# Wider token groups in the gated stage of a one-core attention and expert kernel

## The chip, the core and the metric

The kernel runs on one core of a Trainium2 chip. Its engines are TensorE (PE in the profile; its weight loads are PEld), VectorE (DVE), ScalarE (ACT), GpSimd (POOL) and SyncE (SP), which only issues transfers. The metric is the device time of one execution in microseconds (us).

## What is computed

Three steps follow one another. Attention has 2 batches of 8 heads with 768 tokens of 64 values, masked by hash buckets. Its result, reshaped to 1536 tokens of 512 values, goes through a gated layer with a hidden width of 1536. The outcome goes through a mixture of eight experts, one for each token:

```python
x = attn_out.transpose(0, 2, 1, 3).reshape(B * S, H * D)     # 1536 x 512
y = (x @ w_a) * (x @ w_b) @ w_out                            # w_a, w_b 512 x 1536, w_out 1536 x 512
expert_idx = np.argmax(normalised(y) @ normalised(emb).T / tau, axis=1)
out[mask_e] = gate[mask_e] * (np.maximum(y[mask_e] @ w1[e], 0) @ w2[e])   # w1 512 x 1024, w2 1024 x 512
```

The gated weights arrive as 64-bit floats and are turned into 32-bit ones on the chip.

## The kernel before

All matrix products of the last two steps are made of three: an operand is split into a high part and a low rest of type fp32r, and high x high, high x low and low x high are added in PSUM. Attended values lie in SBUF as such pairs, `xh[b]` and `xl[b]`, a pair of tiles for each batch, 128 x 4 x 768 (four blocks of 128 of the 512 values, by tokens).

**The gated stage** takes the hidden width in six chunks of 256 (`NCH`, chunk `c` from 0 to 5) and the tokens in four groups of 384 (`NG`, group `t`). For each chunk and group, `gated_products` makes `a` and `b` for the two hidden blocks `f` of 128: weight `which` (0 or 1) in two halves of six matmuls, whose moving operand is 384 tokens wide (line 597). When `a` is complete, ScalarE copies it out (606). When `b` is complete, VectorE multiplies (610), ScalarE makes the high part (611) and GpSimd the low one (612), into the tile `g`. `gated_out` then multiplies `g` by the third weight, six matmuls of 512 columns for each block of 128 tokens (629), and VectorE adds the result to `y` (634; in chunk 0 ScalarE copies it, 632). The first half of chunk 0 is done inside attention's last steps.

**The order** is written out by hand in `main`, a list of named steps. For each chunk and group stand the products of `f` = 0, then the outputs of the group before, then the products of `f` = 1. `after` and `chain` hang further jobs on steps of this list: the loading and splitting of the next chunk's weights (`load_gated`, `split64`: seven small jobs on VectorE, ScalarE and GpSimd, of which the fourth adds on GpSimd and the sixth waits for that on VectorE), the router's steps (`route_in` writes 128 rows of `y` to DRAM as `ybuf0` or `ybuf1` for the two batches, and later steps choose experts), and the fetching and splitting of expert weights.

**Expert weights** come in tiles `raw32` of 1 MB: for expert `e`, tile `n` = 0 and 1 are halves of `w1`, 2 and 3 halves of `w2`. Each is split in two halves (`split_expert(e, 0..7)`, lines 879 and 880). After a tile's second half `split` calls `fetch(1)` for the next one. SP issues all these fetches and nine of the twelve `ybuf` writes from one queue, in the order in which they are written down; an instruction that waits holds back all that follow. `gather(e, b)` on GpSimd (885) fetches the rows of batch `b` that expert `e` takes, from `ybuf`, and `transpose_in` (901) turns them on TensorE for `hidden_rows`, `hidden` and `expert_out`.

In attention, `epilogue` (340) has ScalarE copy the value product into the tiles `xp` and `co` of a pair of heads, `finish_add` (344) adds these on GpSimd, and `finish_high` and `finish_low` write `xh` and `xl`.

Of the kernel before, what the change touches and what calls it, by code (L numbers as in the profile page):

```python
# [25 lines left out]
class Kernel:  # L26
# [37 lines left out]
    def attention(self, xh, xl, pools, hook):  # L64
# [9 lines left out]
        for tag, shape, dt, n in (  # L74
            ("et", [128, NC * S], F32, 2), ("e", [128, 2 * S], F32, 3), ("vr", [128, NC * 256], F32, 2), ("raw", [128, 2 * S], F32, 1),
            ("q", [128, S], F32, 2), ("qs", [128, S], F32, 2), ("k", [128, S], F32, 2), ("ks", [128, H2], F32, 2),
            ("xp", [128, S], F32, 2), ("co", [128, S], F32, 2), ("qf", [128, H2], BF16, 2), ("qg", [128, H2], BF16, 2), ("kf", [128, S], BF16, 2), ("sk", [128, H2], BF16, 1),
        ):
            sb.tile(shape, dt, tag=tag, name=tag, bufs=n)
# [250 lines left out]
        def place(i, n, j, g, cs):  # L330
            if i not in XP:
                XP[i] = [sb.tile([128, S], F32, tag=t, name=t, bufs=2) for t in ("xp", "co")]
            x = XP[i][n][64 * j:64 * j + 64, cs.start * 128:cs.stop * 128].rearrange("p (c a s) -> p a c s", a=4, s=32)
            return x[:, 2 * g:2 * g + 2]
# [126 lines left out]
class Experts:  # L461


    def __init__(self, K, const):
# [9 lines left out]
        self.ss, self.lg, self.oh, self.pos, self.gi, self.so, self.gt, self.sg = ({} for _ in range(8))  # L474
        self.yT, self.sel, self.mx, self.rps, self.HS, self.RW = ({} for _ in range(6))


    def split64(self, src, shape, dest, scratch=None):
# [24 lines left out]
        def low():  # L503
            T["r"] = self.conv.tile([128, n], I32, tag="r", name="r64", bufs=2)
            if scratch:
# [74 lines left out]
    def gated_products(self, c, t, f, which, half, psum=None, held=None):  # L580

        nc = self.nc
        b, t2 = divmod(t, 2)
        cols = slice(384 * t2, 384 * (t2 + 1))
        xh, xl = self.xh[b], self.xl[b]
        if f == which == half == 0:
            g = self.mid.tile([128, 4, 384], F32R, tag="g", name="g")
            self.G[c, t] = g[:, 0:2], g[:, 2:4]
        if half == 0:
# [5 lines left out]
        for k in range(half * h, half * h + h):  # L595
            for n, (w, x) in enumerate(((wh, xh), (wh, xl), (wl, xh))):
                nc.tensor.matmul(  # L597
                    p[:, :384], w[:, k, fs], x[:, k, cols],
                    start=(k == 0 and n == 0), stop=(k == self.KD - 1 and n == 2),
                )  # L600
        if half == 0:
            return
        def out():
            if which == 0:
                self.A = self.mid.tile([128, 384], F32, tag="a", name="a")
                nc.scalar.copy(self.A, p[:, :384])  # L606
            else:
                a = self.A
                gh, gl = self.G[c, t]
                nc.vector.tensor_tensor(a, p[:, :384], a, ALU.mult)  # L610
                nc.scalar.copy(gh[:, f], a)  # L611
                nc.gpsimd.tensor_tensor(gl[:, f], a, f32(gh[:, f]), ALU.subtract)  # L612
# [6 lines left out]
    def gated_out(self, c, t, m):  # L619
        nc = self.nc  # L620
        gh, gl = self.G[c, t]
        wh, wl = self.WG[c, 2]
        i = 3 * t + m
        p = self.mm.tile([128, 512], F32, tag="mm", name="yp")
# [240 lines left out]
    def fetch_expert(self, e, n):  # L865

        nc, K = self.nc, self.K
        raw = self.conv.tile([128, 4, 512], F32, tag="raw32", name="raw32", bufs=4)
        src = K.w1[e][:, n * 512:(n + 1) * 512] if n < 2 else K.w2[e][(n - 2) * 512:(n - 1) * 512]
# [223 lines left out]
def tile_kernel(ctx, tc, q, k, v, proj, w_a, w_b, w_out, emb, tau, w1, w2, out, dbg=None):  # L1093
# [5 lines left out]
    with tc.manual_schedule():  # L1099
# [9 lines left out]
        xpool = xctx.enter_context(tc.tile_pool(name="xpool", bufs=1, side="right"))  # L1109
        X.xh = [xpool.tile([128, DM // 128, S], F32R, name=f"xh{b}") for b in range(B)]  # L1110
        X.xl = [xpool.tile([128, DM // 128, S], F32R, name=f"xl{b}") for b in range(B)]
        NG = NT // 384
        NCH = X.F1 // 256
        NU = B * H * (S // 256)
        with tc.tile_pool(name="conv", bufs=1, side="left") as X.conv, \
# [4 lines left out]
            def spare():  # L1120
                return X.mid.tile([128, 4 * 384], F32R, tag="g", name="spare")

# [72 lines left out]
        def outs(c, t):  # L1195
            for m in range(3):
                add(("o", c, t, m), X.gated_out, c, t, m)

        order = [(c, t) for c in range(NCH) for t in range(NG)]
        for s, (c, t) in enumerate(order):  # L1200
# [27 lines left out]
        for c in range(1, NCH):  # L1228
            for w in range(3):
                (fetch, conv), = X.load_gated(c, w, 1)  # L1230
                at = ("p", c - 1, w, 0, 0, 0) if c > 1 else ("o", 0, 0, 0)
                after(at, fetch)
                at = ("p", c - 1, w + 1, 0, 0, 0) if c > 1 or w else ("o", 0, 0, 2)
                chain(at, [[(j,) for j in js] for js in ([conv[0]], [conv[1]], [], conv[2:4], conv[4:6], [conv[6]])], 2 if c > 1 or w else 1)
# [17 lines left out]
        def reopen():  # L1252
            cctx.close()
            X.conv = cctx.enter_context(tc.tile_pool(name="conv3", bufs=1, side="left", reuse_waits="tile"))
            fetch(4)

# [22 lines left out]
        def begin():  # L1279
            xctx.close()  # L1280
            X.ex = xctx.enter_context(tc.tile_pool(name="experts", bufs=1, side="right", reuse_waits="tile"))
            for tag, n in (("xgh", 1024), ("xgl", 1024), ("hs", 1024), ("edge", 72), ("hth", 2048), ("htl", 2048), ("room", 56)):
                X.ex.tile([128, n], F32, tag=tag, name=tag, bufs=1)

        T, R = X.route_in, X.route_logits
# [66 lines left out]
```

## Time and profile before

| | |
|---|---|
| median of 3 runs | 713.81 us (713.38 to 713.83) |
| profiled execution | 712.7 us, of which the span from first to last instruction is 710.9 |
| TensorE busy | 693.8 us, 98% of the span |
| VectorE, GpSimd, ScalarE busy | 453.6, 435.4, 355.7 us (64, 61, 50%) |
| line 597, products of 384 columns | 704 + 352 matmuls recorded outside attention |
| line 629, output products of 512 columns | 432 matmuls |

Attention fills the span to about 200 us, the gated stage from there to about 512, the experts the rest. The busy share of TensorE is drawn from recorded lengths that overlap one another, so a row of starts tells more of its pace. A line of the timeline gives the start and the length of one or several merged instructions, then engine, line, operation, tiles (written <- read), shapes, and their number. A line of the chain of waits gives the start, the length and the work that the end of the execution waited for.

### The profile page before, as it was taken

The numbers are of one execution on the slowest core, as the hardware profiler recorded it, in microseconds if no ns is written. First come the engines' busy times: TensorE is split into PE (matmuls) and PEld (weight loads), VectorE is DVE, ScalarE is ACT, GpSimd is POOL, SyncE is SP. The second block draws the span as 40 slices with busy tenths as digits, with TensorE's granted clock in tenths as the row PEclk, the third lists the DMA queues.
The fourth block names the chain that finished last, engine by engine and source line by source line (L and its number), as shares of the span: only waits on it lengthen the run. The fifth ranks groups of instructions, "written<-read, shape, count | busy, mean of one in ns | idle before, by whom it ended". The sixth has DMA issues, their size and how long they took to land.

```text
span 710.9 us, 16289 instructions
## 1 busy us (share of the span) xinstructions
PE 693.8 (98%) x6796; PEld 583.5 (82%) x6796; DVE 453.6 (64%) x623; ACT 355.7 (50%) x660; POOL 435.4 (61%) x439
## 2 busy tenths in 40 slices
PE   8899999999999999999999999999999999999996
PEld 5465656566689999999999999988889899989995
DVE  4899999999966636546546456335646756556640
ACT  4789888988744341211212121234546565555560
POOL 1789999989964735636726537454525766657651
PEclk9999999999999999999999999999999999999999
DMA  6947754743241311211303201633533865676500
GB/s 151 211 106 182 162 126 116 171 114 96 47 136 60 120 61 60 67 52 60 119 0 108 71 12 48 234 108 104 169 110 101 284 229 197 205 258 226 208 37 24
DMA packets 68444, 88.00 MB, mean 124 GB/s; under 512 B 28931, under 2 KB 41027, under 8 KB 68368
## 3 DMA queue, kind: packets, MB, share of 16 engines
q1 hardware_dynamic: 63728, 78.41, 37.4%
q0 software_dynamic: 2560, 7.34, 2.7%
q10 hardware_dynamic: 2080, 1.18, 0.6%
q8 instruction: 54, 0.88, 0.5%
q14 instruction: 22, 0.18, 0.1%
HBM read 75.52 MB, written 7.34 MB: 117 GB/s over the span
## 4 chain that ended last, share of the span: by engine, by line
PE 82%; DVE 6%; ACT 5%; issue 3%; DMA 2%; POOL 2%; SPq 0%; POOLq 0%; ACTq 0%; DVEq 0%
PE ab L597 26%; PE yp L629 14%; PE op L974 11%; PE hp L924 10%; PE pv L320 8%; PE st L270 5%; DVE nm L278 3%; ACT e L284 2%; DVE et L308 2%; PE part L597 1%; PE st L273 1%; PE hr L942 1%; PE xgt L901 1%; ACT xp L340 1%; ACT co L340 1%
## 5 line engine op out<-in xcount | busy, mean ns | idle before, releaser
L597 PE MATMUL ab<-xh,w 128*128 128x384 f32 x704 | 185.7, 338 | 0.0
L597 PEld LDWEIGHTS ab<-xh,w 128*128 128x128 f32 x704 | 127.7, 188 | 2.0 <-issue 1.2
L597 PE MATMUL ab<-xl,w 128*128 128x384 f32 x352 | 118.3, 336 | 0.0
L612 POOL TENSOR_TENSOR g<-a,g 128x384 fp32r<-128x384 f32 x48 | 52.5, 1094 | 102.1 <-ACT g L611 101.9
L880 POOL TENSOR_TENSOR w<-raw,w 128x1024 fp32r<-128x1024 f32 x36 | 87.9, 2446 | 38.7 <-ACT w L879 37.2
L629 PE MATMUL yp<-w,g 128*128 128x512 f32 x432 | 102.9, 390 | 0.0
L301 POOL TENSOR_SCALAR e<-e,r,mc 128x768 f32<-128x768 f32 x96 | 93.7, 983 | 10.2 <-DVE r L288 10.0
L284 ACT ACTIVATE e<-st,nm 128x768 f32<-128x768 f32 x96 | 85.7, 896 | 27.4 <-DVE r L288 14.6
L278 DVE TENSOR_REDUCE nm<-st 128x1 f32<-128x768 f32 x96 | 90.0, 943 | 11.4 <-PE st L273 11.3
L629 PEld LDWEIGHTS yp<-w,g 128*128 128x128 f32 x432 | 80.4, 188 | 14.9
L270 PE MATMUL st<-k,q 64*128 64x384 f32 x192 | 83.4, 515 | 2.2 <-ACT e L284 1.9
L308 DVE STREAM_TRANSPOSE et<-e 128x1536 f32<-128x1536 f32 x48 | 84.8, 1768 | 0.0
L270 PE MATMUL st<-ks,qs 64*128 64x384 f32 x192 | 82.8, 511 | 1.9 <-ACT e L284 1.8
L974 PE MATMUL op<-w,hth 128*128 128x512 f32 x256 | 80.7, 396 | 0.0
L924 PE MATMUL hp<-xgh,w 128*128 128x256 f32 x448 | 80.7, 281 | 0.0
L611 ACT CAST g<-a 128x384 fp32r<-128x384 f32 x48 | 24.7, 515 | 111.5 <-DVE a L610 111.5
L320 PEld LDWEIGHTS pv<-et,vr 32*64 32x64 f32 x3072 | 60.2, 130 | 17.9 <-issue 8.7
L320 PE MATMUL pv<-et,vr 32*64 32x192 f32 x3072 | 72.5, 326 | 2.0 <-ACT q L128 1.6
L880 DVE TENSOR_TENSOR w<-raw,w 128x1024 fp32r<-128x1024 f32 x28 | 64.6, 2309 | 14.6 <-ACT w L879 14.6
L924 PEld LDWEIGHTS hp<-xgh,w 128*128 128x128 f32 x448 | 69.2, 188 | 0.3
L606 ACT COPY a<-ab 128x384 f32<-128x384 f32 x44 | 21.0, 476 | 95.1 <-PE ab L597 93.8
L597 PEld LDWEIGHTS ab<-xl,w 128*128 128x128 f32 x352 | 66.2, 188 | 0.8
(218 smaller groups left out, 1243.9 us busy)
## 6 DMA issues: line engine op xcount, KB each, us to landing
raw<-in_moe_w_dram SPq DMA_DIRECT2D x32, 1024.0 KB, 5.3
vr<-in_v_dram SPq DMA_DIRECT2D x64, 192.0 KB, 3.8
raw<-in_moe_w_a_dram SPq DMA_DIRECT2D x5, 1024.0 KB, 5.1
raw<-in_moe_w_b_dram SPq DMA_DIRECT2D x5, 1024.0 KB, 4.9
raw<-in_moe_w_out_dram SPq DMA_DIRECT2D x5, 1024.0 KB, 4.8
raw<-in_k_dram SPq DMA_DIRECT2D x16, 192.0 KB, 4.0
qs<-q SPq DMA_DIRECT2D x15, 192.0 KB, 3.8
raw<-in_q_dram SPq DMA_DIRECT2D x14, 192.0 KB, 4.1
```

What stands on the lines that cost most here:

```text
L270: nc.tensor.matmul(st[:, n, :H2], q[d, ql], k[d], start=True, stop=False, tile_position=(64 * n, 0))
L278: nc.vector.tensor_reduce(NM[u][:, t:t + 1], ST[u, t][:, :, :H2], axis=AX.XY, op=ALU.max, negate=True)
L284: nc.scalar.activation(halves(E[u][:, t]), ST.pop((u, t))[:, :, :H2], AF.Exp, bias=NM[u][:, t:t + 1], accum_out=SU[u][:, t:t + 1])
L301: nc.gpsimd.tensor_scalar(E[u][:, t], E[u][:, t], r[:, t:t + 1], c[:, t:t + 1], ALU.mult, ALU.add)
L308: nc.vector.transpose(ET[h][:, :, 2 * g:2 * g + 2].rearrange("p b c s -> p c b s"), E.pop(u).rearrange("p c (b s) -> p c b s", s=32),)
L320: nc.tensor.matmul(pvb[a // 2][m:m + 64, a % 2, :NC * 32], v[d], et[d, n].rearrange("p c s -> p (c s)"), start=(n < 2), stop=(n >= NB32 - ...
L597: nc.tensor.matmul(p[:, :384], w[:, k, fs], x[:, k, cols], start=(k == 0 and n == 0), stop=(k == self.KD - 1 and n == 2),)
L612: nc.gpsimd.tensor_tensor(gl[:, f], a, f32(gh[:, f]), ALU.subtract)
L629: nc.tensor.matmul(p, g[:, f, rows], w[:, f], start=(n == 0), stop=(n == 5))
L880: eng.tensor_tensor(l, raw, f32(h), ALU.subtract)
L924: nc.tensor.matmul(p[:, :256], w[:, k, fs], x[:, k], start=(n == 0), stop=(n == 3 * self.KD - 1))
L974: nc.tensor.matmul(p, h[:, 2 * n + f, rows], w[:, f], start=(n == 0 and f == 0 and m == 0), stop=(n == 3 and f == 1 and m == 2),)
```

## The change

Chunks 1 to 4 take the tokens in three groups of 512; chunks 0 and 5 keep four groups of 384. A group of 512 crosses from one batch to the other, so `xh` and `xl` become one tile each for both batches, and `g` and `a` become 512 wide. The room for that comes from elsewhere: one buffer of `co` in place of two, one of the scratch tile `r` in place of two, and three of the four `raw32` buffers from the start, with the fourth (pool `conv4`) opened only when the attended values are released (`begin`). A `Ring` takes the `raw32` buffers in turn. The jobs that split the next chunk's weights are placed by position in the chunk's list of steps.

```diff
-            ("xp", [128, S], F32, 2), ("co", [128, S], F32, 2), ...
+            ("xp", [128, S], F32, 2), ("co", [128, S], F32, 1), ...
...
+        self.raws = Ring()
+
+    def width(self, c):
+        return 512 if 0 < c < self.F1 // 256 - 1 else 384
...
-            T["r"] = self.conv.tile([128, n], I32, tag="r", name="r64", bufs=2)
+            T["r"] = self.conv.tile([128, n], I32, tag="r", name="r64", bufs=1)
...
-        b, t2 = divmod(t, 2)
-        cols = slice(384 * t2, 384 * (t2 + 1))
-        xh, xl = self.xh[b], self.xl[b]
+        n = self.width(c)
+        cols = slice(n * t, n * (t + 1))
+        xh, xl = self.xs
...
                 nc.tensor.matmul(
-                    p[:, :384], w[:, k, fs], x[:, k, cols],
+                    p[:, :n], w[:, k, fs], x[:, k, cols],
...
-        raw = self.conv.tile([128, 4, 512], F32, tag="raw32", name="raw32", bufs=4)
+        raw = self.raws.tile([128, 4, 512], F32, tag="raw32", name="raw32")
...
-            for m in range(3):
+            for m in range(X.width(c) // 128):
                 add(("o", c, t, m), X.gated_out, c, t, m)
 
-        order = [(c, t) for c in range(NCH) for t in range(NG)]
+        order = [(c, t) for c in range(NCH) for t in range(NT // X.width(c))]
...
-                at = ("p", c - 1, w, 0, 0, 0) if c > 1 else ("o", 0, 0, 0)
-                after(at, fetch)
-                at = ("p", c - 1, w + 1, 0, 0, 0) if c > 1 or w else ("o", 0, 0, 2)
+                at = ("p", c - 1, w + 1, 0, 0, 0) if w else ("o", 0, 0, 2)
+                if c > 1:
+                    first = next(i for i, m in enumerate(main) if m[0] == ("p", c - 1, 0, 0, 0, 0))
+                    at = main[first + 10 * w + 5][0]
+                after(main[first + (0, 9, 19)[w]][0] if c > 1 else ("o", 0, 0, 0), fetch)
...
-            X.conv = cctx.enter_context(tc.tile_pool(name="conv3", bufs=1, side="left", reuse_waits="tile"))
-            fetch(4)
+            X.raws.add(cctx.enter_context(tc.tile_pool(name="conv3", bufs=3, side="left", reuse_waits="tile")), 3)
+            fetch(3)
...
+            X.raws.add(cctx.enter_context(tc.tile_pool(name="conv4", bufs=1, side="left", reuse_waits="tile")), 1)
+            fetch(1)
```

On TensorE, around the outputs of a group in chunk 1 (`ab` are the products, `yp` the outputs, `w` the weights), before:

```order
L597 MATMUL ab<-xh_99,w 128x384 x2
L597 MATMUL ab<-xl_101,w 128x384
L597 MATMUL ab<-xh_99,w 128x384
L629 MATMUL yp<-w,g 128x512 x18
L597 MATMUL ab<-xh_99,w 128x384
```

and now:

```order
L601 MATMUL ab<-xh,w 128x512 x2
L601 MATMUL ab<-xl,w 128x512
L601 MATMUL ab<-xh,w 128x512
L633 MATMUL yp<-w,g 128x512 x24
L601 MATMUL ab<-xh,w 128x512
```

The products are 512 wide, and four blocks of 128 tokens are put out in a row in place of three.

On SP's queue at the end of the gated stage, with numbered tiles, before (`raw32_5908` is tile 1 of expert 1, `raw32_6133` and `raw32_6241` its tiles 2 and 3, `raw32_6576` tile 0 of expert 2; `ybuf0` and `ybuf1` are the rows of the two batches):

```order
L870 DMA raw32_5908<-in_moe2_w1_dram 128x4x512
L692 DMA ybuf0_68<-y_3760 128x512 x2
L870 DMA raw32_6133<-in_moe2_w2_dram 128x4x512
L692 DMA ybuf1_69<-y_3760 128x512 x3
L870 DMA raw32_6241<-in_moe2_w2_dram 128x4x512
L870 DMA raw32_6576<-in_moe2_w1_dram 128x4x512
```

and now (`raw32_5654` is tile 0 of expert 1, `raw32_5863` its tile 1, `raw32_5884` and `raw32_5992` its tiles 2 and 3):

```order
L874 DMA raw32_5654<-in_moe2_w1_dram 128x4x512
L696 DMA ybuf0_68<-y_3760 128x512 x2
L874 DMA raw32_5863<-in_moe2_w1_dram 128x4x512
L874 DMA raw32_5884<-in_moe2_w2_dram 128x4x512
L696 DMA ybuf1_69<-y_3760 128x512 x3
L874 DMA raw32_5992<-in_moe2_w2_dram 128x4x512
```

Each fetch stands one place later, and two of them now precede the three writes of `ybuf1`. Of the three buffers in turn, `raw32_5863` gets the one of expert 0's tile 2, which its second half's split (`split_expert(0, 5)`) frees, and `raw32_5884` the one of expert 0's tile 3, which `split_expert(0, 7)` frees. Before, four buffers in turn gave `raw32_6133` the one that `split_expert(0, 5)` frees, and `raw32_6241` the one that `split_expert(0, 7)` frees.

## Rows read from the trace of the kernel before

**Rows 1.** The page: granted TensorE clock in 40 slices, in tenths of full speed.

```profile
PEclk9999999999999999999999999999999999999999
```

**Rows 2.** Waits of TensorE, 196 to 520 us: us in total, times, longest.

```profile
PE pv L320 <- ACT a L606: 0.4, 1, 0.4
```

**Rows 3.** Timeline of TensorE, 323 to 332 us: start, length, instruction.

```profile
323.70 0.34 PE L597 MATMUL ab<-xl,w 128*128 128x384 f32 x1
...
326.82 0.34 PE L597 MATMUL ab<-xl,w 128*128 128x384 f32 x1
...
327.69 4.24 PE L629 MATMUL yp<-w,g 128*128 128x512 f32 x18
331.77 0.34 PE L597 MATMUL ab<-xh,w 128*128 128x384 f32 x1
```

**Rows 4.** Timeline of TensorE, 600 to 603 us, among the experts.

```profile
600.77 0.63 PE L974 MATMUL op<-w,hth 128*128 128x512 f32 x2
...
602.86 0.39 PE L974 MATMUL op<-w,hth 128*128 128x512 f32 x1
```

**Rows 5.** Timeline of four engines, 337 to 341 us.

```profile
337.43 0.55 DVE L610 TENSOR_TENSOR a<-ab,a 128x384 f32<-128x384 f32 x1
...
338.01 0.52 ACT L611 CAST g<-a 128x384 fp32r<-128x384 f32 x1 [3.42 <-DVE a L610]
...
338.60 1.02 POOL L612 TENSOR_TENSOR g<-a,g 128x384 fp32r<-128x384 f32 x1 [2.35 <-ACT g L611]
...
340.10 1.07 PE L629 MATMUL yp<-w,g 128*128 128x512 f32 x4
```

**Rows 6.** Timeline of GpSimd and ScalarE in attention, an earlier pair and the last.

```profile
63.39 1.00 POOL L344 TENSOR_TENSOR xp<-xp,co 128x384 f32<-128x384 f32 x1
...
66.13 0.47 ACT L340 COPY co<-pv 64x384 f32<-64x384 f32 x1
...
206.21 1.01 POOL L344 TENSOR_TENSOR xp<-xp,co 128x384 f32<-128x384 f32 x1
...
207.16 0.48 ACT L340 COPY co<-pv 64x384 f32<-64x384 f32 x1
```

**Rows 7.** Timeline of SP, VectorE, GpSimd and TensorE, 216 to 251 us.

```profile
216.53 0.38 SPq L492 DMA_DIRECT2D raw<-in_moe_w_b_dram  x1
...
217.62 1.03 DVE L352 TENSOR_TENSOR xl<-xp,xh 128x384 fp32r<-128x384 f32 x2 [0.58 <-ACT xh L348]
...
240.75 3.36 POOL L528 TENSOR_TENSOR w<-v,w 128x1024 fp32r<-128x1024 f32 x1
...
250.45 0.51 PE L597 MATMUL ab<-xh,w 128*128 128x384 f32 x2
```

**Rows 8.** Timeline of SP's queue, 505 to 520 us.

```profile
505.42 0.38 SPq L870 DMA_DIRECT2D raw<-in_moe_w_dram  x1
505.90 1.85 SPq L692 DMA_DIRECT2D ybuf<-y  x3
516.71 0.38 SPq L870 DMA_DIRECT2D raw<-in_moe_w_dram  x1
```

**Rows 9.** Timeline of GpSimd, 500 to 530 us.

```profile
514.30 2.38 POOL L880 TENSOR_TENSOR w<-raw,w 128x1024 fp32r<-128x1024 f32 x1 [5.42 <-ACT w L879]
524.20 0.96 POOL L885 DMA_INDIRECT xg<-ybuf,gi  x1 [7.52 <-DVE oif L831]
```

**Rows 10.** The chain of waits, 500 to 560 us: start, length, what.

```profile
524.23 3.45 PE op L974 x15
...
527.71 0.63 PE xgt L901 x4
```

**Rows 11.** DMAs issued at 506.9 to 508 us: size, us to landing.

```profile
ybuf<-y SPq DMA_DIRECT2D x1, 256.0 KB, 7.0
xg<-ybuf,gi POOLq DMA_INDIRECT x1, 6.7
```

**Rows 12.** DMAs issued at 524 to 525 us: the gather.

```profile
xg<-ybuf,gi POOLq DMA_INDIRECT x1, 3.4
```

More of the change, by code (lines that the diff above doesn't have):

```diff
@@ L76, in attention @@
             ("q", [128, S], F32, 2), ("qs", [128, S], F32, 2), ("k", [128, S], F32, 2), ("ks", [128, H2], F32, 2),
[L77 removed]
+            ("xp", [128, S], F32, 2), ("co", [128, S], F32, 1), ("qf", [128, H2], BF16, 2), ("qg", [128, H2], BF16, 2), ("kf", [128, S], BF16, 2), ("sk", [128, H2], BF16, 1),
         ):
@@ L331, in place @@
             if i not in XP:
-                XP[i] = [sb.tile([128, S], F32, tag=t, name=t, bufs=2) for t in ("xp", "co")]
+                XP[i] = [sb.tile([128, S], F32, tag=t, name=t, bufs=n) for t, n in (("xp", 2), ("co", 1))]
             x = XP[i][n][64 * j:64 * j + 64, cs.start * 128:cs.stop * 128].rearrange("p (c a s) -> p a c s", a=4, s=32)
@@ L582, in gated_products @@
         nc = self.nc
-        b, t2 = divmod(t, 2)
-        cols = slice(384 * t2, 384 * (t2 + 1))
-        xh, xl = self.xh[b], self.xl[b]
+        n = self.width(c)
+        cols = slice(n * t, n * (t + 1))
+        xh, xl = self.xs
         if f == which == half == 0:
-            g = self.mid.tile([128, 4, 384], F32R, tag="g", name="g")
-            self.G[c, t] = g[:, 0:2], g[:, 2:4]
+            g = self.mid.tile([128, 4, 512], F32R, tag="g", name="g")
+            self.G[c, t] = g[:, 0:2, :n], g[:, 2:4, :n]
         if half == 0:
@@ L595, in gated_products @@
         for k in range(half * h, half * h + h):
-            for n, (w, x) in enumerate(((wh, xh), (wh, xl), (wl, xh))):
+            for m, (w, x) in enumerate(((wh, xh), (wh, xl), (wl, xh))):
                 nc.tensor.matmul(
-                    p[:, :384], w[:, k, fs], x[:, k, cols],
-                    start=(k == 0 and n == 0), stop=(k == self.KD - 1 and n == 2),
+                    p[:, :n], w[:, k, fs], x[:, k, cols],
+                    start=(k == 0 and m == 0), stop=(k == self.KD - 1 and m == 2),
                 )
@@ L604, in out @@
             if which == 0:
-                self.A = self.mid.tile([128, 384], F32, tag="a", name="a")
-                nc.scalar.copy(self.A, p[:, :384])
+                self.A = self.mid.tile([128, 512], F32, tag="a", name="a")[:, :n]
+                nc.scalar.copy(self.A, p[:, :n])
             else:
@@ L609, in out @@
                 gh, gl = self.G[c, t]
-                nc.vector.tensor_tensor(a, p[:, :384], a, ALU.mult)
+                nc.vector.tensor_tensor(a, p[:, :n], a, ALU.mult)
                 nc.scalar.copy(gh[:, f], a)
@@ L622, in gated_out @@
         wh, wl = self.WG[c, 2]
-        i = 3 * t + m
+        i = self.width(c) // 128 * t + m
         p = self.mm.tile([128, 512], F32, tag="mm", name="yp")
@@ L1109, in tile_kernel @@
         xpool = xctx.enter_context(tc.tile_pool(name="xpool", bufs=1, side="right"))
-        X.xh = [xpool.tile([128, DM // 128, S], F32R, name=f"xh{b}") for b in range(B)]
-        X.xl = [xpool.tile([128, DM // 128, S], F32R, name=f"xl{b}") for b in range(B)]
-        NG = NT // 384
+        X.xs = [xpool.tile([128, DM // 128, NT], F32R, name=t) for t in ("xh", "xl")]
+        X.xh, X.xl = [[x[:, :, b * S:(b + 1) * S] for b in range(B)] for x in X.xs]
+        for tag, shape in (("g", [128, 4, 512]), ("a", [128, 512])):
+            X.mid.tile(shape, F32, tag=tag, name=tag)
         NCH = X.F1 // 256
@@ L1120, in spare @@
             def spare():
-                return X.mid.tile([128, 4 * 384], F32R, tag="g", name="spare")
+                return X.mid.tile([128, 4 * 512], F32R, tag="g", name="spare")
             def late():
```

## Prediction

> **What bounds the kernel now.** I read first who waited for whom on TensorE between 196 and 520 us, the stretch that holds the gated stage. One wait of 0.4 us stands there, and it is of attention's value product (line 320), so still in attention's tail [rows 2]. In the gated stage itself the other engines hide behind TensorE, and a change there is worth what it takes off TensorE's own row of matmuls. The granted clock reads 9 tenths or more in all forty slices of the page [rows 1], which is the level of 2.4 GHz throughout.
>
> Next I read that row at the finest grain. A matmul's recorded length (0.34 us at 384 columns) overlaps the next one's, so the price is the distance between starts. From 323.70 to 326.82 us lie 18 matmuls of 384 columns: 3.12 / 18 = 173.3 ns each. From 327.69 to 331.77 us lie 18 of 512 columns, those of the output projection: 4.08 / 18 = 226.7 ns [rows 3]. The difference, 53.4 ns, is 128 columns at 2.4 GHz. What is left over is the same at both widths, 173.3 - 160.0 = 13.3 ns and 226.7 - 213.3 = 13.4 ns. A matmul here costs its columns plus a fixed 13.3 ns, and only the number of matmuls can be saved.
>
> **The main term.** A gated chunk has 2 hidden blocks x 2 weights x 12 = 48 product matmuls for each group of tokens. Four groups of 384 make 192, three of 512 make 144. The columns stay the same (73,728), and the 72 output matmuls stay as they are.
> - before: 192 x 173.3 ns = 33.27 us for each chunk
> - after: 144 x 226.7 ns = 32.64 us
> - saved: 0.63 us, and in chunks 1 to 4 together 2.5 us.
>
> Chunks 0 and 5 keep 384, so nothing changes in them. The price at 512 columns is taken from another line (L629) of the same stage, with the same kind of operands. The dearest spacing at this width that I found is among the experts' matmuls, 600.77 to 602.86 us: 2.09 / 9 = 232.2 ns [rows 4]. With that the four chunks would lose 4 x (144 x 232.2 - 33,270) ns = 0.7 us. I take 226.7, since the output matmuls stand between the very products that are widened; the other end goes to the rivals.
>
> **What hides the rest of the gated stage.** ScalarE, VectorE and GpSimd do as many columns as before in three instructions in place of four, so their work shrinks. What grows is the time to hand one group on: VectorE 0.55, ScalarE 0.52, GpSimd 1.02 us, at most a third more each, 0.7 us together. Before, that subtraction ends at 339.62 us, and the first reader of its half is the sixth output matmul, at 340.10 + 5 x 0.2267 = 341.23: 1.6 us to spare [rows 5]. The 24 products that stand between now take 24 x 226.7 = 5.44 us in place of 4.16, so the room grows by 1.28 and the need by 0.7. Cost nothing. The jobs that split the next chunk's weights are dealt out anew; an addition on GpSimd followed by a VectorE job that waits for it still fits into one group's products, and should that fail, the first to be late would be a PSUM buffer's release, some tenths of a us in each chunk.
>
> **Buffers taken away.** Each may add a wait.
> - One "co" tile: ScalarE's copy now waits until GpSimd has added the pair before. In the row of an earlier pair the addition ends at 64.39 and the copy starts at 66.13, so 1.7 us are spare. At the last pair the addition ends at 207.22 and the copy starts at 207.16 [rows 6]. About 0.1 us, with TensorE at work on products there. Queued behind it on ScalarE are three more copies; 0 to 0.1 us, taken as 0.
> - The load of chunk 1's second weight now waits for VectorE's last attention subtraction (ends 218.65) and not for GpSimd's, after which it was issued at 216.53: 2.1 us later. Its last split starts on GpSimd at 240.75 for 3.36 us, ending at 244.1, and its first product is the second of the pair at 250.45, so 6 us are spare [rows 7]. One "r" scratch tile: its next writer already stands behind the addition that frees it. Both cost nothing.
> - Three raw buffers for expert weights until attention's values are released, a fourth only then. This one is not free.
>
> **The new wait.** SP's queue runs in order. Before, it fetched one tile at 505.42, when a split on GpSimd had freed a buffer, and behind it wrote three row blocks of the second batch to DRAM, from 505.90. It then fetched the next tile at 516.71, when the split that starts at 514.30 had ended [rows 8, 9]. With three buffers in rotation an extra fetch stands at 505.4, and the one that stands directly ahead of the three writes is given the buffer which only the split at 514.30 to 516.68 frees. So the three writes leave 11 us later, with one fetch directly ahead of them and another directly behind. Waiting for them is the gather of the second batch, issued on GpSimd at 524.20 [rows 9] and landed 3.4 us later [rows 12], at 527.6. TensorE's transpose of what it brings starts at 527.71, right after its previous matmul [rows 10]. That hand-over has no room: what the gather loses, TensorE loses.
>
> How late? In the clock of before: the last of the three writes was issued at 506.9 and landed 7.0 us later [rows 11], 8.5 us after the fetch ahead of it was issued. From 516.71 that gives 525.2, 1.0 us after the gather is ready. The other end is 0, since this case also had ScalarE's writes and a gather in flight. On top of that the gather may share the DMA engines with the fetch behind the writes. Quiet it took 3.4 us; issued just behind such traffic it took 6.7 [rows 11, 12]: 0 to 3.3 more. I take 0.6 us for both, near the quiet end, because that fetch is issued some 5 us ahead of the gather and should be nearly through. Bounds: 0 and 4.3 us.
>
> The Trainium skill ("DMA: Bandwidth & Descriptors", "Queues, rings and completion order") says that each DMA engine goes round-robin, packet by packet, between the queues that have work. By it the gather would be slowed by sharing but not held until SP's fetch is done, and the 3.3 us would not be reached. The 6.7 us of the trace speak rather for a longer hold.
>
> **The sum.** The profiled execution took 712.7 us (span 710.9): 712.7 - 2.5 + 0.6 = 710.8. It lies 1.1 below the median of the runs, 713.81, so the change is put to the median: 713.81 - 1.9 = 711.9 us.
>
> **Rivals.**
> - *The writes land in time.* All rows as above, but 7.0 us shrinks since ScalarE's writes are gone from that moment. 713.81 - 2.5 = 711.3; with some tenths either way 711.0 to 711.5.
> - *The gather is caught.* Writes 1.0 us late, and the gather as slow as the slow one of the two [rows 11]: up to 4.3 late, 713.81 - 2.5 + 4.3 = 715.6, slower than before. It eats the whole gain from 2.5 us on. For it speaks that nothing on TensorE gives a lost us back there [rows 10]; against it, that the two fetches and three writes have some 7 us to get through. Most of its weight lies between 1.5 and 3.5 us late, 712.8 to 714.8.
> - *The fixed price isn't saved.* The wide products run at 232.2 ns [rows 4]: 713.81 + 0.7 + 0.6 = 715.1. Against it: nothing in the gated stage's own row of matmuls runs so [rows 3].
> - *A price of 2.5 ns.* A fixed part of 2.5 ns in place of 13.3 would leave 192 x 2.5 ns = 0.5 us to save: 713.81 - 0.5 + 0.6 = 713.9. The Trainium skill ("TensorE: Matmul & The Clock Gate", "Back-to-back issue gap") gives that: columns / 2.4 GHz plus about 2.5 ns, 215.7 at 512. The trace disagrees at both widths, with 13.3 and 13.4, so this gets almost no chance.
>
> That the change does not do what it says is ruled out by the order of its instructions: 128x512 products, with 24 output matmuls in a row between them.
>
> **How the numbers follow.** My forecast (0.1 to 1.4 us late, 711.3 to 712.7) has 0.52; writes in time 0.17; gather caught 0.22, of which 0.06 beyond 4.0 us late; price not saved 0.05; 2.5 ns 0.02; something unseen 0.02. A measurement of this kernel can tell about 0.2% (1.4 us) from no change, so faster means below 712.4. Of my forecast nearly all is there (0.48), and the writes-in-time case whole: faster 0.65. Same: the rest of the forecast, most of the caught gather, the prices: 0.27. Slower: 0.08. The range goes from 711.0, the lower end of the first rival, to 713.9, in the middle of the second: some 0.03 are left out below and 0.16 above.
>
> **What would show it.** In chunks 1 to 4 of the changed kernel: product starts 226.7 ns apart and a chunk of 48.96 us (144 + 72 matmuls). On SP's queue: a fetch, three writes and a fetch back to back at about 514.2 us. On TensorE: a gap of about 0.6 us ahead of the gathered rows' transpose, near 525. I am wrong if the spacing exceeds 230 ns, if that gap exceeds 1.5 us, or if a wait of TensorE appears between 210 and 500 us.

## The result, and the profile after

The changed kernel takes 718.96 us (median of 6 runs, 717.18 to 719.1), the kernel before 713.82 (6 runs beside it, 713.38 to 715.87). The ratio is 1.0059, interval 1.0043 to 1.0075: **slower** by 3 to 5 us, where 711.9 was forecast and the range ended at 713.9.

The profiled execution took 719.09 us (before: 712.7), with a span of 717.3 (before 710.9), 6.4 us more. The first step is to find in which stretch they lie. On TensorE's timeline four starts mark the stages: the first output matmul (yp), the last gated product (ab), the first output matmul of expert 0 (op), and the first hidden matmul of expert 1 (hp). The changed kernel's rows (start, length, engine, line, instruction):

```profile
220.63 0.62 PE L633 MATMUL yp<-w,g 128*128 128x512 f32 x2
...
502.29 0.34 PE L601 MATMUL ab<-xh,w 128*128 128x384 f32 x1
...
524.04 0.63 PE L978 MATMUL op<-w,hth 128*128 128x512 f32 x2
...
549.30 0.28 PE L928 MATMUL hp<-xgh,w 128*128 128x256 f32 x1
```

The same four marks read from every kernel's trace (us; the experiments are told below):

| kernel | up to yp | yp to last ab | last ab to op | op to hp | hp to the end |
|---|---|---|---|---|---|
| before | 219.64 | 280.21 | 21.75 | 21.33 | 167.98 |
| changed | 220.63 | 281.66 | 21.75 | 25.26 | 167.99 |
| e1_order | 219.94 | 281.67 | 21.75 | 21.37 | 167.97 |
| e2_pad | 221.78 | 282.30 | 21.80 | 25.28 | 168.04 |
| e3_narrow | 220.47 | 281.23 | 21.75 | 24.72 | 168.03 |
| e4_align | 219.28 | 278.12 | 21.81 | 24.97 | 167.99 |
| e5_both | 219.80 | 278.10 | 21.81 | 21.31 | 167.99 |
| e6_ring | 222.33 | 280.22 | 21.76 | 24.63 | 168.02 |
| e7_fill | 220.12 | 281.68 | 21.75 | 23.64 | 167.98 |
| e8_swap | 221.12 | 281.67 | 21.75 | 21.41 | 167.98 |

The first column is attention. It differs by up to 3 us between profiles with no pattern in the kernels (219.28 to 222.33). The latest is that of e6_ring, whose attention is that of before; there the granted clock stood at 0.50 from 35.0 to 38.4 us. The changed kernel lies inside this spread, so its 0.99 us are taken as one execution's chance. Two columns differ by cause: the chunks, **+1.45 us** where -2.5 was forecast, and the stretch from op to hp, **+3.93 us** where +0.6 was forecast. Together 5.38 us in this execution, against 5.14 between the medians and 3.1 to 5.4 by the interval of the ratio.

**The chunks.** From 298.21 to 303.81 us lie eight groups of three products; the output matmuls behind them begin at 304.27, the next product at 309.74. The rows have the same form as above:

```profile
298.21 0.40 PE L601 MATMUL ab<-xl,w 128*128 128x512 f32 x1
...
303.81 0.40 PE L601 MATMUL ab<-xl,w 128*128 128x512 f32 x1
...
304.27 5.63 PE L633 MATMUL yp<-w,g 128*128 128x512 f32 x24
...
309.74 0.40 PE L601 MATMUL ab<-xh,w 128*128 128x512 f32 x1
```

24 products in 5.60 us are 233.3 ns each, 6.6 ns above the 226.7 of [rows 3]. The spacing holds in all groups of the four chunks. The 24 output matmuls, of the same 512 columns, take 5.47 / 24 = 227.9 on average: the first five are slow (230, 236, 228, 233, 231), the rest run at 226 or 227. So the width is not slow in itself, and the products' operands come under suspicion.

**The gather.** The waits of TensorE from 222 us to the end hold one line, which the kernel before does not have (us in total, times, longest); then the timeline of SP's queue, of GpSimd and of TensorE around it (in brackets the idle time before an instruction and what ended it):

```profile
PE xgt L905 <- DMA xg<-ybuf,gi: 2.4, 1, 2.4
```
```profile
507.54 11.99 SPq L874 DMA_DIRECT2D raw<-in_moe_w_dram  x2
519.62 1.94 SPq L696 DMA_DIRECT2D ybuf<-y  x3
521.65 0.72 SPq L874 DMA_DIRECT2D raw<-in_moe_w_dram  x1
```
```profile
516.74 2.38 POOL L884 TENSOR_TENSOR w<-raw,w 128x1024 fp32r<-128x1024 f32 x1 [5.76 <-ACT w L883]
...
528.70 0.96 POOL L889 DMA_INDIRECT xg<-ybuf,gi  x1 [9.57 <-DVE htl L965]
```
```profile
529.74 0.39 PE L978 MATMUL op<-w,htl 128*128 128x512 f32 x1
532.57 0.63 PE L905 MATMUL xgt<-ident,xg 128*128 128x128 f32 x4 [2.44 <-DMA xg<-ybuf,gi]
```

The first SP row is two fetches; the second of them is held until the split on GpSimd ends (516.74 + 2.38 = 519.12), and the three row-block writes stand behind it until 519.62. In [rows 8] they were issued at 505.90. The gather behind them starts 4.66 us after op (528.70 - 524.04); in [rows 9] it started 524.20 - 521.60 = 2.60 us after it. So it is 2.06 us later, it takes 3.74 us to landing in place of 3.38, and TensorE has nothing else to do.

**The clock.** The same place in windows (from:to, length, busy time and count of PE, PEld, DVE, ACT, POOL, then granted clock, DMA share, GB/s):

```profile
532.00:533.00 1.00, 0.43 (x5) 0.46 (x5) 0.00 (x0) 0.00 (x0) 0.00 (x0) 1.00 0.00 0
533.00:534.00 1.00, 1.00 (x6) 0.54 (x4) 0.14 (x1) 0.65 (x2) 0.53 (x1) 0.93 0.00 0
534.00:535.00 1.00, 1.00 (x5) 1.00 (x6) 0.66 (x2) 0.98 (x2) 0.51 (x2) 0.50 0.00 0
535.00:536.00 1.00, 1.00 (x7) 1.00 (x7) 0.00 (x0) 0.99 (x2) 0.94 (x1) 0.50 0.78 213
536.00:537.00 1.00, 1.00 (x6) 1.00 (x6) 0.68 (x4) 0.18 (x1) 0.00 (x0) 0.50 0.57 217
537.00:538.00 1.00, 1.00 (x10) 1.00 (x9) 0.49 (x3) 0.00 (x0) 0.00 (x0) 0.87 0.09 33
```

After the wait the granted clock is 0.50 (1.2 GHz) for some 3.4 us (the shortfalls add to 0.07 + 3 x 0.50 + 0.13 = 1.70 us at the most). The stretch from op to hp grew by 3.93; less the wait of 2.44 that leaves 1.49 us. That fits a clock at half for that long, if some of the time wasn't spent on matmuls. In the kernel before this stretch shows 1.00 throughout.

### The profile page after: what moved, and what is told of

It is laid out like the page before. It is cut to its first block, busy times and chain, and to the rows that moved or that the text cites. A ratio compares the mean times of both kernels' runs of the same rounds, so it can differ in the third digit from the quotient of the medians.

```text
span 717.3 us, 15868 instructions
## 1 busy us (share of the span) xinstructions
PE 696.6 (97%) x6604; PEld 559.7 (78%) x6604; DVE 454.3 (63%) x615; ACT 354.3 (49%) x644; POOL 434.3 (61%) x431
## 4 chain that ended last, share of the span: by engine, by line
PE 79%; DVE 6%; ACT 5%; POOL 4%; issue 4%; DMA 3%; SPq 0%; POOLq 0%; ACTq 0%; DVEq 0%
PE ab L601 26%; PE yp L633 14%; PE op L978 10%; PE hp L928 10%; PE pv L320 6%; PE st L270 4%; DVE nm L278 3%; ACT e L284 2%; POOL e L301 2%; DVE et L308 2%; PE part L601 1%; PE hr L946 1%; PE st L273 1%; PE xgt L905 1%; PE pv L601 1%
## 5 line engine op out<-in xcount | busy, mean ns | idle before, releaser
L601 PE MATMUL ab<-xh,w 128*128 128x512 f32 (+1 forms) x576 | 175.3, 378 | 0.0
L616 POOL TENSOR_TENSOR g<-a,g 128x512 fp32r<-128x512 f32 (+1 forms) x40 | 56.6, 1415 | 112.6 <-ACT g L615 112.6
L601 PEld LDWEIGHTS ab<-xh,w 128*128 128x128 f32 x576 | 107.1, 188 | 18.8 <-issue 1.3
L601 PE MATMUL ab<-xl,w 128*128 128x512 f32 (+1 forms) x288 | 108.2, 376 | 0.0
L615 ACT CAST g<-a 128x512 fp32r<-128x512 f32 (+1 forms) x40 | 23.2, 579 | 111.5 <-DVE a L614 111.5
L610 ACT COPY a<-ab 128x512 f32<-128x512 f32 (+1 forms) x36 | 19.8, 550 | 98.0 <-PE ab L601 94.1
L614 DVE TENSOR_TENSOR a<-ab,a 128x512 f32<-128x512 f32 (+1 forms) x36 | 23.2, 646 | 70.2 <-PE ab L601 69.8
```

The lines of the kernel that those rows point to most:

```text
L601: nc.tensor.matmul(p[:, :n], w[:, k, fs], x[:, k, cols], start=(k == 0 and m == 0), stop=(k == self.KD - 1 and m == 2),)
```

## The experiments

Each kernel's time is compared, as a ratio, with the kernel before, run on the same chip in the same minutes. The two probes carry extra work, so only their rows are read.

### e1_order: the fetch takes the free buffer

```diff
-            X.raws.add(cctx.enter_context(tc.tile_pool(name="conv4", bufs=1, side="left", reuse_waits="tile")), 1)
+            X.raws.slots.insert(2, cctx.enter_context(tc.tile_pool(name="conv4", bufs=1, side="left", reuse_waits="tile")))
             fetch(1)
```

> The changed kernel with one line altered: the fourth raw buffer enters the rotation at the place of its first use, so that the fetch ahead of the three row-block writes of the second batch takes the new buffer and waits only for the last gated product. If the wait of SP's queue holds the gather up (2.4 us of wait on TensorE, and then 1.5 us in which the granted clock is below full), the wait of the gathered rows' transpose goes and the clock stays up: 718.96 - 2.4 - 1.5 = 715.1 us, of which up to 1.5 may remain if the fall of the clock has another cause (716.6). Rival, the gather is slow because it shares the DMA engines with fetches: the writes land early, the transpose still waits some 2 us, about 718.5 us. The product spacing stays 233.3 ns in both.

Measured: 715.74 us (12 runs), ratio 1.0018 (1.0002 to 1.0033). No wait of TensorE is left after 222 us, the clock is 1.00 from 520 to 560, and op to hp takes 21.37 us, as before. SP's queue:

```profile
506.87 0.93 SPq L874 DMA_DIRECT2D raw<-in_moe_w_dram  x2
507.89 1.62 SPq L696 DMA_DIRECT2D ybuf<-y  x3
518.46 0.38 SPq L874 DMA_DIRECT2D raw<-in_moe_w_dram  x1
```

So the second stretch's 3.93 us come from the place of one fetch in the queue. What is left is the chunks' 1.46 us.

### e3_narrow: groups of 384 everywhere

```diff
-        return 512 if 0 < c < self.F1 // 256 - 1 else 384
+        return 384
```

> The changed kernel with groups of 384 in all chunks; the merged tiles, the single buffers and the rotation of 3 + 1 raw buffers stay. The products then cost 173.3 ns each as before. If the loss in the chunks (1.45 us) is the spacing of the wide products alone, this takes 718.96 - 1.45 = 717.5 us, with the gather's wait of about 2.4 us and the fall of the clock still there. Rival, the merged tiles or the single buffers cost time in the chunks: a wait or a spacing above 173.4 ns shows there, and the time stays at 719.

Measured: 718.05 us (7 runs), 1.0036 (1.0019 to 1.0053). Products run at 173.4 ns again in all chunks. The stretch of the chunks still takes 281.23 us, 1.02 above before. Of these, 0.97 us are lost at one place, between the product rows that start at 282.97 and 296.35 (13.38 us, before 12.41), where an output matmul waits for GpSimd's g:

```profile
289.39 2.41 POOL L515 TENSOR_TENSOR v<-v,r 128x1024 int32<-128x1024 int32 x1 [2.43 <-DVE r L512]
291.76 1.45 POOL L616 TENSOR_TENSOR g<-a,g 128x384 fp32r<-128x384 f32 x1
```
```profile
293.26 3.02 PE L633 MATMUL yp<-w,g 128*128 128x512 f32 x12 [0.67 <-POOL g L616]
```

An addition for the next chunk's weights stands directly ahead of the subtraction that makes g; the places of these jobs were dealt out for three groups. Elsewhere in the stretch only 0.05 us are lost, so the merged tiles and the single buffers cost next to nothing there. Op to hp is 24.72, so the late gather does not need the wide groups. That the 1.45 us of the change are the spacing alone this run does not prove, since its own wait took the place of the gain; e5_both does.

### e2_pad and p1_probe: which part of the operands

```diff
         X.xh, X.xl = [[x[:, :, b * S:(b + 1) * S] for b in range(B)] for x in X.xs]
+        xpool.tile([128, 8], F32, name="pad")
```

> The changed kernel with 32 bytes of padding, so that the tiles xh and xl start on a multiple of 64 bytes (180160 and 204736 in place of 180192 and 204768); w's tiles, which the output projection reads at 226.7 ns a matmul, start on such multiples. If the start address makes the 512-wide products slow (233.3 ns in place of 226.7), they run at 226.7: 4 x 144 x 6.67 ns = 3.8 us less, 715.1 us. Rival, the distance of 24,576 bytes between xh and xl or anything else in the operands: no change, 233.3 ns, 719.0 us. The gather's wait stays 2.4 us in both.

Measured: 720.18 us (6 runs), 1.0069 (1.0046 to 1.0091). The wide products stay at 233.3 ns and the gather's wait at 2.5 us. The products of 384 columns in chunks 0 and 5, though, went from 173.4 to 176.7 ns: from 234.39 to 237.57 us 18 of them take 3.18 us. The theory of a multiple of 64 falls. That a shift of 32 bytes changes the price at all suggests that the start address matters.

The probe puts rows of 24 matmuls into the chunks, each of which changes one thing:

```diff
...
+                terms = [(wh[:, k, fs], xh[:, k, cols]), (wh[:, k, fs], xl[:, k, cols]), (wl[:, k, fs], xh[:, k, cols])]
+                if v == 1:
+                    terms = [(a, xh[:, k, cols]) for a, _ in terms]
...
+                elif v == 3:
+                    terms = [(wh[:, k, fs], oh[:, f]), (wh[:, k, fs], ol[:, f]), (wl[:, k, fs], oh[:, f])]
...
                 products(c, t, 1)
+                if 1 < c < NCH - 1:
+                    for v in range(2):
+                        add(("v", c, t, v), X.probe, c, order[s - 1], 2 * (3 * (c - 2) + t) + v)
```

> The changed kernel with 18 extra rows of 24 matmuls in chunks 2 to 4, two behind each group's products, into a PSUM tile that nobody reads; the time grows by them and says nothing. Each row changes one thing against the product (weights high, high, low; tokens high, low, high; 512 columns): row 0, 16, 17 nothing; 1 only xh; 2 only one k of xh; 3 the output weights as moving operand; 4 stationary g; 5 stationary only the high part; 6 one stationary block; 7 stationary g and moving output weights, as the output projection; 8 to 10 448, 480 and 496 columns; 11 to 15 starts shifted by 32, 64, 96, 512 and 1024 bytes. If the start address decides, rows 3, 7, 11 and 13 run at 226.7 ns and the others of 512 columns at 233.3; if the moving tiles' distance decides, rows 1, 2, 3 and 7 run at 226.7; if the stationary operand decides, rows 4 and 7, perhaps 5 and 6. The widths tell whether the surplus of 6.7 ns begins below 512 columns: 448 / 2.4 + 13.3 = 200.0, 480: 213.3, 496: 220.0 ns without it.

Measured, mean start-to-start distance of the twelve matmuls ahead of the last one in each row (ns):

| row | what differs | ns |
|---|---|---|
| 0, 16, 17 | nothing | 233.3 |
| 1 | only xh | 233.3 |
| 2 | one k of xh | 233.3 |
| 3 | output weights as moving operand | 226.7 |
| 4 | stationary g | 233.3 |
| 5, 6 | stationary high part; one block | 233.3 |
| 7 | stationary g, moving output weights | 226.7 |
| 8, 9, 10 | 448, 480, 496 columns | 204.4, 220.0, 226.2 |
| 11 | start shifted by 32 bytes | 226.7 |
| 12 | 64 bytes | 233.3 |
| 13 | 96 bytes | 228.9 |
| 14, 15 | 512, 1024 bytes | 233.3 |

The stationary operand and the alternation of xh and xl change nothing. The moving operand's address does: row 11 reads the same tiles as row 0, 32 bytes on. The widths show a surplus above columns plus 13.3 ns already at 448 columns (4.4 ns), and one of 6.2 to 6.7 from 480 on.

### p2_probe: all starts

The same rows, with `n, off = (512, 384, 256)[v // 8], 8 * (v % 8)`.

> The changed kernel with 18 extra rows of 24 matmuls as in p1_probe; the time says nothing. Rows 0 to 7: 512 columns with the start of the moving operand shifted by 0, 32, ... 224 bytes, that is 224, 0, 32, 64, 96, 128, 160, 192 bytes past a multiple of 256. Rows 8 to 15 the same with 384 columns, rows 16 and 17 with 256 columns at 224 and 0. If a multiple of 256 is what makes 512 columns fast, row 1 alone runs at 226.7; if a multiple of 128 does, row 5 too; if of 64, rows 3 and 7 too (row 3 was 228.9). For 384 columns the starts known are 224 (173.3) and 192 (176.7).

Rows 0 and 1 follow each other on TensorE's timeline; twelve matmuls lie between each pair of starts:

```profile
316.18 0.63 PE L638 MATMUL pb<-xh,w 128*128 128x512 f32 x2
...
318.98 0.63 PE L638 MATMUL pb<-xh,w 128*128 128x512 f32 x2
...
321.75 0.62 PE L638 MATMUL pb<-xh,w 128*128 128x512 f32 x2
...
324.47 0.62 PE L638 MATMUL pb<-xh,w 128*128 128x512 f32 x2
```

2.80 / 12 = 233.3 ns and 2.72 / 12 = 226.7. All starts, as bytes past a multiple of 256, with the distance as above (ns):

| start past 256 | 0 | 32 | 64 | 96 | 128 | 160 | 192 | 224 |
|---|---|---|---|---|---|---|---|---|
| 512 columns | 226.7 | 233.3 | 228.9 | 233.3 | 233.3 | 234.2 | 233.3 | 233.3 |
| 384 columns | 173.3 | 176.7 | 173.3 | 176.7 | 175.8 | 173.3 | 174.6 | 173.3 |
| 256 columns | 120.0 | | | | | | | 118.3 |

With 512 columns only a multiple of 256 gives 226.7; 64 bytes past one comes near (228.9). As built, the changed kernel's tiles start at 180192 and 204768, 224 past a multiple; every group's offset (2,048 bytes) keeps that. With 384 columns 224 is as good as 0, and the kernel before, whose tiles start at 224 too, showed no surplus. The weights' tiles start on multiples of 256 (20224 and 28416, for instance), and the output matmuls that gave the forecast its price read these.

### e5_both and e4_align: the tiles moved to a multiple of 256

```diff
+        xpool.tile([128, 56], F32, name="pad")
```

e4_align is the changed kernel with this line alone, e5_both has it and the line of e1_order.

> The changed kernel with the rotation of e1_order and 224 bytes of padding, so that xh and xl start on multiples of 256 bytes (179968 and 204544). The probe's row with a shift of 32 bytes (start 180224, a multiple of 256) ran at 226.7 ns, the one of 96 bytes (64 past a multiple) at 228.9, all others of 512 columns from these tiles at 233.3. If the start address is what counts, the wide products run at 226.7: 4 x 144 x 6.67 = 3.8 us under e1_order, which measured 1.0018 of the kernel before, so about 0.9965 of it, 711.3 us where the kernel before takes 713.8. Rival, the probe's rows ran fast for another reason (place in the program, other engines' work): 233.3 ns in the chunks and 1.0018. Open in both: what this start does to the products of 384 columns in chunks 0 and 5, which went from 173.3 to 176.7 ns with the start of e2_pad.

> The changed kernel with 224 bytes of padding alone (xh and xl on multiples of 256 bytes), the rotation of the raw buffers as in the change. If the address and the queue are two separate causes, the spacing goes to 226.7 ns (3.8 us less than the changed kernel) and the gather's wait of 2.4 us and the fall of the clock stay: 1.0059 - 0.0054 = 1.0005 of the kernel before. Rival, the loss in the chunks hides part of the gather's wait or makes it: then the wait on TensorE changes by more than 0.3 us.

Measured: e5_both 710.68 us (12 runs), **0.9960** (0.9948 to 0.9973), faster than both kernels; e4_align 713.54 us (12 runs), 1.0001 (0.9985 to 1.0017). In e5_both 24 products take 5.44 us, 226.7 ns each, and so do the 24 output matmuls that follow a row of such products (318.86 to 324.30; the changed kernel took 5.47):

```profile
308.21 0.39 PE L601 MATMUL ab<-xl,w 128*128 128x512 f32 x1
...
313.65 0.39 PE L601 MATMUL ab<-xl,w 128*128 128x512 f32 x1
...
318.86 5.60 PE L633 MATMUL yp<-w,g 128*128 128x512 f32 x24
324.30 0.39 PE L601 MATMUL ab<-xh,w 128*128 128x512 f32 x1
```

The chunks take 278.10 and 278.12 us in the two, 2.1 us under before and 3.55 under the change; e4_align keeps the gather's wait (2.4 us) and e5_both has none. The two causes are separate and add.

Read closer, e5_both takes 208.96 us from the product row in which the width first changes to the row behind the one in which it changes back (244.69 to 453.65); before, the same stretch took 211.46 (244.38 to 455.84), and in the changed kernel 212.91 (245.37 to 458.28). That is -2.50 us in chunks 1 to 4, as the sum had it. In the rest, chunks 0 and 5 with 384 columns, e5_both loses 0.39: its narrow products stand at 173.9 ns in place of 173.4, and the short rows of 12 and 6 among other work cost some ns more each.

### e6_ring: only the queue's part, in the kernel before

```diff
+        self.raws = Ring()
...
-        raw = self.conv.tile([128, 4, 512], F32, tag="raw32", name="raw32", bufs=4)
+        raw = self.raws.tile([128, 4, 512], F32, tag="raw32", name="raw32")
...
-            X.conv = cctx.enter_context(tc.tile_pool(name="conv3", bufs=1, side="left", reuse_waits="tile"))
-            fetch(4)
+            X.raws.add(cctx.enter_context(tc.tile_pool(name="conv3", bufs=3, side="left", reuse_waits="tile")), 3)
+            fetch(3)
...
+            X.raws.add(cctx.enter_context(tc.tile_pool(name="conv4", bufs=1, side="left", reuse_waits="tile")), 1)
+            fetch(1)
```

> The kernel before with one part of the change alone: three raw buffers in rotation and a fourth that joins when attention's values are released, the fetch of it issued there; groups stay at 384. If the order of SP's queue makes the gather late by itself, TensorE waits 2.1 to 2.5 us for the gathered rows and the granted clock falls behind that wait for some 1.5 us of loss: 713.8 + 3.9 = 717.7 us, 1.0055 of the kernel before. Rival, the wait needs the wide chunks (other times of the splits): no wait, 1.000.

Measured: 716.57 us (12 runs), 1.0041 (1.0027 to 1.0056). Its profile has the wait and behind it the clock:

```profile
PE xgt L902 <- DMA xg<-ybuf,gi: 1.9, 1, 1.9
```
```profile
533.00:536.00 3.00, 3.00 (x14) 2.57 (x13) 0.81 (x2) 2.71 (x4) 1.98 (x2) 0.56 0.28 85
```

Op to hp grew by 3.30 us: 1.9 of wait, and the other 1.4 are put down to the clock. The rival (no wait without the wide chunks) falls. The 1.0055 expected lies at the upper end of the interval; its wait was half a us too long.

### e8_swap: the writes ahead of the late fetch

```diff
             X.raws.add(cctx.enter_context(tc.tile_pool(name="conv4", bufs=1, side="left", reuse_waits="tile")), 1)
-            fetch(1)
...
-        chain(("o", L, 2, 1), [(T, 6), (T, 7), (T, 8), (GL, 2), (GT, 2)])
+        chain(("o", L, 2, 1), [(T, 6), (T, 7), [(T, 8), (fetch, 1)], (GL, 2), (GT, 2)])
```

> The changed kernel with the late fetch of expert weights issued behind the three row-block writes of the second batch in place of ahead of them; the fetch still waits for the split on GpSimd (about 519 us in the changed kernel's clock) and a second one still follows it. If the gather was late because the writes landed late, it is issued 2.1 us earlier and the wait on TensorE goes to 0.4 us or less, the clock stays up: 2.0 to 2.4 + 1.5 us less, about 715.3 us, 1.0010 of the kernel before. Rival, the gather is slowed by sharing the DMA engines with the two fetches: they are both still there just ahead of it, so it takes 5 us or more in place of 3.4 to 3.7 and TensorE waits 1.5 us or more.

Measured: 714.48 us (11 runs), 1.0020 (1.0010 to 1.0031). SP's queue, and the gather as a DMA (us to landing):

```profile
508.52 2.13 SPq L696 DMA_DIRECT2D ybuf<-y  x3
519.65 0.93 SPq L874 DMA_DIRECT2D raw<-in_moe_w_dram  x2
```
```profile
xg<-ybuf,gi POOLq DMA_INDIRECT x1, 3.5
```

The two fetches are as late as in the changed kernel (the first 4.89 us ahead of op in both), the gather is issued 2.58 us after op (527.12 - 524.54) and takes 3.5 us, and TensorE waits for nothing. So what held the gather up in the changed kernel was the writes, not sharing. The GpSimd row of the changed kernel names a VectorE job as what ended its wait (528.03), because that ended last by the profile, just behind the writes' landing (527.93). The gather doesn't need that job: here it is issued at 527.12, and the job ends at 528.50.

```profile
527.81 0.69 DVE L965 TENSOR_TENSOR htl<-ht,hth 128x512 fp32r<-128x512 f32 x1 [0.49 <-ACT hth L964]
```

### e7_fill: work in the gap

```diff
...
+        after(("e", 0, 0, "half"), X.fill, 10)
         after(("e", 0, 0, "half"), X.transpose_in, 0, 1)
```

> The changed kernel with 10 extra matmuls of 512 columns (into a PSUM tile that nobody reads) on TensorE just ahead of the transpose that waits 2.4 us for the gathered rows; nothing of the computation is left out. They fill the wait (10 x 0.227 = 2.3 us). If the clock falls to 0.50 because TensorE stood idle for 2.4 us, it stays at 1.00 now, and the 3.1 us at half speed give back about 1.5 us: 718.96 - 1.5 = 717.4, 1.0038 of the kernel before. Rival, the clock falls at this place for another reason: still 0.50 for some 3 us, 1.0059.

Measured: 716.77 us (6 runs), 1.0055 (1.0039 to 1.0071). By the time alone this is unclear: the interval just misses 1.0038 and holds 1.0059. The traces say more. The filler and the transpose, and the window behind:

```profile
529.45 2.43 PE L627 MATMUL fl<-w 128*128 128x512 f32 x10
531.99 0.63 PE L911 MATMUL xgt<-ident,xg 128*128 128x128 f32 x4
```
```profile
533.00:537.00 4.00, 4.00 (x33) 3.71 (x32) 1.98 (x8) 3.00 (x5) 1.87 (x2) 1.00 0.35 116
```

In the changed kernel the same window has 19 matmuls at a mean clock of 0.61:

```profile
533.00:537.00 4.00, 4.00 (x19) 3.54 (x18) 1.49 (x6) 2.80 (x4) 1.97 (x2) 0.61 0.34 108
```

The gather is issued just as late here (528.22, 4.67 us after op). Op to hp is 23.64 in place of 25.26; of these 1.62 us 0.1 is the gather's, which took 3.64 us in place of 3.74, and the rest the clock's.

That TensorE's idleness brought the clock down this run alone does not show. In p2_probe nothing fills the gap, TensorE waits as long, and yet the clock stays up and op to hp is 23.64 too:

```profile
PE xgt L922 <- DMA xg<-ybuf,gi: 2.4, 1, 2.4
```
```profile
616.00:620.00 4.00, 4.00 (x32) 3.59 (x31) 1.77 (x7) 3.00 (x5) 1.98 (x2) 1.00 0.35 116
```

Taken together, the clock fell behind the unfilled wait in six of seven profiles (changed kernel, e2_pad, e3_narrow, e4_align, e6_ring and p1_probe, not p2_probe), and at this place in none of the five without the wait or with the gap filled (before, e1_order, e5_both, e8_swap, e7_fill). So the fall goes with the idle gap, but the gap does not always bring it; what decides stays open.

## Why the prediction was wrong, point by point

- **The main term** (-2.5 us) failed in one step: the price of a wide product was taken from the output matmuls [rows 3] on the ground that they have the same kind of operands and the same place. They have not the same start address of the moving operand. At 233.3 ns the four chunks cost 4 x (144 x 233.3 - 33,270) ns = +1.3 us; measured +1.45. The counting of matmuls, the columns and the unchanged chunks were right: with the tiles moved (e5_both) chunks 1 to 4 shrink by 2.50 us, as forecast. That chunks 0 and 5 stay as they are holds in the changed kernel and not at the moved start, where they lose 0.39.
- **The rival with the right number** was the third, "the fixed price isn't saved" (232.2 ns, +0.7 us), given 0.05. What spoke against it, that nothing in the gated stage's own row of matmuls runs so, was true only of matmuls that read other addresses or other widths. The slow rows that it rested on [rows 4] are something else: the first matmuls behind a row that reads xgh and xgl, which start at 196064 and 200160, again 224 past a multiple of 256. The probe's rows 3 and 7, behind rows at 224, begin with 230, 236, 229 ns and come down to 226.7 after five matmuls, row 11 after ten. Behind the changed kernel's products the output matmuls begin so too, and behind the moved tiles of e5_both they don't (226 and 227 ns from the first). So a row is slow for a while behind a badly placed one; why stays open. That the mean of such a start, 232.2, lies so near 233.3 is luck.
- **The price of 2.5 ns** was rightly given almost no chance: no row read here, once it has settled, comes under 13.3 ns above the columns at 512 and 384, and the probes' rows of 512 have 13.3 to 21. The Trainium skill ("TensorE: Matmul & The Clock Gate", "Back-to-back issue gap") states columns / 2.4 GHz plus 2.5 ns as the gap of a single matmul by itself, and not for a stream of weight loads and matmuls as here, so it was not the rule to hold against these rows.
- **The new wait** was found, with its place and its queue, and it was mis-sized. The sum had 1.0 us late from the writes (landing at 525.2 against a gather ready at 524.2) and then took 0.6 for that and for sharing together, less than its own first part. Measured in the clock of before (2.44 us are taken off, op to op): the last write landed at 525.5, 0.3 later; from the landing to the gather's issue passed 0.77 us, which the sum left out; the gather took 3.74 in place of 3.38. 1.0 + 0.3 + 0.77 + 0.36 = 2.43 us. The rival "the gather is caught" (1.5 to 3.5 us) had this, at 0.22, and largely for another reason: of the 3.3 us that it allowed for sharing, 0.36 came. How queues that are both full share the DMA engines is decided by no run: when the changed kernel's gather was issued the traffic was running out (408 GB/s from 528 to 529 us, 109 from 530 to 531), and the late gathers took 3.4 to 3.7 us. The Trainium skill ("DMA: Bandwidth & Descriptors", "Queues, rings and completion order") has the queues take turns packet by packet. No run here tells that from the longer hold that the prediction set against it.
- **What the wait sets off** was not in the sum at all: 1.5 us of clock behind 2.4 us of wait in the profiled execution. The prediction counted a us lost by TensorE as one us, so even "gather caught" at its centre would have come out low. The wait alone does not settle whether an execution pays it, as p2_probe shows.
- **What costs nothing** held: for the single co tile, the single r tile, the load of chunk 1's second weight and the longer hand-over no wait of TensorE shows in the changed kernel. Between 222 and 530 us it has none, and from 196 to 222 us the 0.4 us of [rows 2] and 0.2 us in which it waited for nothing that the profile shows.
- **The sum.** Forecast -2.5 + 0.6; measured +1.45 + 2.44 + 1.49 = +5.4. Curing one of the two misses does not make the kernel faster: e4_align, without the slow spacing, comes out even (1.0001), and e1_order, without the wait, slower by 0.2%; e5_both, without either, is faster by 0.4%. Of the three signs of being wrong that the prediction's last paragraph names, two came (a spacing above 230 ns, a gap above 1.5 us).

## What to carry to other kernels

A price per instruction read from a neighbouring line holds only if everything that the instruction reads is alike, the start address too: before a tile is widened, look where the moving operand starts, and put it on a multiple of 256 bytes if the matmuls are 512 wide. When buffers are taken from a rotation, follow the queue that fills them in order: what stands behind the fetch that must now wait is what the change costs. And where TensorE will stand idle for some 2 us, allow for the clock behind it: here some 1.5 us more, in six of seven profiles.

## What the runs showed of the hardware

- The distance of two matmuls depends on the start address of the moving operand: 226.7 to 234.2 ns at 512 columns, 173.3 to 176.7 at 384, over shifts of 32 bytes (p2_probe). Multiples of 256 bytes were the only start with 226.7 at 512. Why the address matters stays open. The Trainium skill ("SBUF — State Buffer", "Operand start alignment") asks for a multiple of the element size only, and says that this is about legality and not speed. All starts here are such multiples; the runs add their price in time.
- Behind a row that reads a badly placed operand, a row of 512 columns on a well placed one starts slowly: 24 output matmuls took 5.47 us in the changed kernel and 5.44 in e5_both.
- At 256 columns the order is turned round: 118.3 ns at 224 past a multiple, 120.0 on one. And one start did not give one price at 384: 192 past a multiple took 174.6 ns in the probe and 176.7 in e2_pad's chunks. What the rows around it add stays open too.
- After waits of TensorE of 1.9 to 2.5 us for the gather the granted clock fell to 0.50 (1.2 GHz) for some 3.4 us in six profiles (changed kernel, e2_pad, e3_narrow, e4_align, e6_ring, p1_probe). In a seventh, with a wait of 2.35 us (p2_probe), it stayed at 1.00, as it did at that place without the wait or with it filled (before, e1_order, e5_both, e7_fill, e8_swap).
- From the landing of the last write to the issue of the gather that waited for it passed 0.76 to 0.77 us in all eight profiles in which it waited.
